# Transposes of q, k and x moved from TensorE to DMA, in a sliding-window attention followed by an MLP

## Chip, cores, metric

One core of one Trainium2 chip. All kernels of one comparison ran on the same chip beside the kernel before; the experiments used two chips, with medians of the kernel before of 362.0 to 362.5. SP below is SyncE, whose queue issues stores and DMA transposes; PSUM is where TensorE's products land; an eviction is ScalarE's copy of a finished PSUM bank to SBUF; the granted clock is TensorE's clock as a share of full speed.

## What is computed

```python
B, H, S, D = 8, 8, 576, 64
scores = q @ k.transpose(0, 1, 3, 2) / 8          # kept where 0 <= query - key < 64
attn   = softmax(scores) @ v
x      = attn.transpose(0, 2, 1, 3).reshape(4608, 512)
h      = x @ w_in                                  # 512 -> 2048
out    = (h - tanh(h)) @ w_out                     # 2048 -> 512
```

Inputs and output are float32; the kernel computes in bf16.

## The kernel before

The MLP runs in nine chunks of 512 tokens. A script counts half steps: an even one issues the four matmuls of `hp_mm` for one sixteenth of a chunk, an odd one the four of `yp_mm`, and attention work of later batches is put between them. A batch has 32 half steps. The parts that matter here:

```python
    def tr(g, which, bank, *engs):            # q or k of one pair of heads, on TensorE
        ...
        for e in range(E):
            nc.tensor.transpose(tp[:, e, :], src[:, e, :], ident[:P, :P])
        ...                                   # then copied from PSUM by ScalarE or VectorE
    def y_out(c, s):                          # one PSUM bank: the next yp_mm waits for this
        ysb = sm_pool.tile([128, d_model], F32, tag="ysb", name="ysb")
        nc.scalar.activation(ysb, ps[:, yp_bank(c, s), :], ACT.Copy)
        ...
    for g in range(3 * NP, B * NP):           # pairs of heads from the fourth batch on
        b, pr = divmod(g, NP)
        a = 8 * g - 48
        at(a - 7, cast, g, "q")
        at(a - 5, cast, g, "k")
        at(a, tr, g, "q", 3, nc.scalar, nc.vector)
        at(a + 2, tr, g, "k", 3, nc.scalar)
        for i in range(3):
            at(a + 5 + 2 * i, scores, g, i, 4)
        ...
        if pr % 2 == 1:
            at(a + 20, x_tr, b, pr // 2, 0, 4, 3)
            at(a + 22, x_tr, b, pr // 2, 4, NJ, 3)
        if pr == 0:
            at(32 * b - 78, load_v_all, b)    # GpSimd's software queue, casts f32 to bf16
            at(32 * b - 64, load_all, b, "q")
            at(32 * b - 63, load_all, b, "k")
    ...
        if h % 2 == 0:                        # order inside a half step
            if sy % 4 == 0 and 0 < n - LAG <= 16 * NC:
                y_out(*divmod((n - LAG) // 4 - 1, 4))
            if 0 <= c < NC:
                hidden = hp_mm(c, m)
        elif 0 <= cy < NC:
            yp_mm(cy, sy)
        for fn in items.get(h, []):
            fn[0](*fn[1:])
```

The softmax here doesn't subtract the row's maximum and nothing guards it: scores larger than these inputs give would overflow.

## Time and profile before

| | before |
|---|---|
| median, later runs of the same comparison included | 361.9 us |
| TensorE busy | 326.2 us of 362.1 |
| hardware-issued DMA | 17.69 MB |
| software-issued DMA (loads with a cast) | 17.90 MB |

The prediction shows the lines that tell what bounds it.

And one line in order of time, the eviction of y that precedes the q transposes at 151.46 us which the prediction shows:

```profile
151.19 0.59 ACT L283 ACTIVATE ysb<-ps 128x512 f32<-128x512 f32 x1
```

It ends at 151.78; the MLP matmuls that write the same PSUM bank start at 151.83.

### The profile page before, as it was taken

The page shows a single profiled execution, that of the slowest core. Times are in us where ns is not written, and L with a number is a line of the kernel's source. Part 1 is how long each engine was busy: PE and PEld are TensorE (multiplying, and loading weights), DVE is VectorE, ACT ScalarE, POOL GpSimd, SP SyncE. Part 2 cuts the span into 40 slices and gives each one's busy share as a digit, 9 for nine tenths or more (in the row PEclk, how much of TensorE's full clock was granted, in tenths as well). Part 3 has the DMA queues.
Part 4 walks back from the last instruction along what each step waited for, and adds up shares of the span by engine and source line. Part 5 has one row for each costly group of instructions (what it writes and reads, how often), then busy time and mean ns, then how long its engine had stood idle before and what let it go on. Part 6 is the DMA issues. An engine that isn't in the chain of part 4 may idle for free.

```text
span 362.1 us, 6043 instructions
## 1 busy us (share of the span) xinstructions
PE 326.2 (90%) x2329; PEld 189.5 (52%) x2329; DVE 214.7 (59%) x352; ACT 192.8 (53%) x355; POOL 103.6 (29%) x136
## 2 busy tenths in 40 slices
PE   0538667889999999999999999999999999999995
PEld 0438345655555555555555555555555544444442
DVE  3418657775676776767677767677676633443300
ACT  2536364876656656565656555655564444443421
POOL 7809522806319309312830272110000000000000
PEclk9999998999999999999999999999999999999999
DMA  8899992377876567655935592250000010010012
GB/s 158 128 218 200 216 222 54 54 137 114 202 155 92 97 163 123 129 99 121 139 84 108 128 129 74 58 127 31 30 32 29 31 58 29 31 57 29 31 67 78
DMA packets 31948, 36.76 MB, mean 102 GB/s; under 512 B 3472, under 2 KB 25872, under 8 KB 31536
## 3 DMA queue, kind: packets, MB, share of 16 engines
q0 software_dynamic: 20384, 17.90, 32.7%
q1 hardware_dynamic: 10904, 17.69, 17.0%
q10 hardware_dynamic: 632, 0.79, 0.7%
q8 instruction: 18, 0.29, 0.4%
q14 instruction: 10, 0.08, 0.1%
HBM read 36.70 MB, written 9.44 MB: 127 GB/s over the span
## 4 chain that ended last, share of the span: by engine, by line
PE 73%; DMA 15%; issue 5%; POOL 3%; ACT 2%; DVE 2%; SPq 0%; POOLq 0%; ACTq 0%; DVEq 0%
PE ps L278 32%; PE ps L259 29%; DMA vw<-vb 7%; DMA kall<-in_k_dram 4%; PE ps L224 4%; PE ps L197 3%; PE ps L210 3%; DMA vall<-in_v_dram 2%; PE ps L241 2%; DMA vw<-vw 1%; POOL kb L81 1%; POOL vb L81 1%; DVE qt L81 1%; ACT th L262 1%; POOL qb L81 0%
## 5 line engine op out<-in xcount | busy, mean ns | idle before, releaser
L259 PE MATMUL ps<-xT,wi 128*128 128x512 bf16 x576 | 148.2, 381 | 1.0 <-DVE gT L268 0.9
L278 PE MATMUL ps<-w_out_sb,gT 128*128 128x512 bf16 x576 | 145.2, 379 | 0.2 <-ACT ysb L283 0.2
L268 DVE TENSOR_TENSOR gT<-ps,th 128x512 bf16<-128x512 f32 x144 | 98.9, 690 | 74.2 <-ACT th L262 73.0
L262 ACT ACTIVATE th<-ps 128x512 f32<-128x512 f32 x144 | 86.0, 598 | 85.4 <-PE ps L259 84.1
L259 PEld LDWEIGHTS <-wi 128*128 128x128 bf16 x576 | 61.3, 114 | 47.0 <-issue 2.7
L278 PEld LDWEIGHTS <-gT 128*128 128x128 bf16 x576 | 53.6, 98 | 51.3 <-issue 0.5
L214 ACT ACTIVATE pt<-ps 128x384 bf16<-128x384 f32 x96 | 46.9, 491 | 48.5 <-PE ps L210 37.7
L81 POOL COPY vb<-vall 72x1024 bf16<-72x1024 bf16 x28 | 29.4, 1060 | 71.3 <-DMA vw<-vb 53.9
L235 DVE TENSOR_TENSOR xs<-ps,rc 64x576 bf16<-64x576 f32 x64 | 48.3, 755 | 1.5
L210 PE MATMUL ps<-qt,kt 128*128 128x128 bf16 x288 | 37.3, 230 | 5.6 <-ACT pt L214 3.1
L224 PE MATMUL ps<-vw,pt 128*128 128x130 bf16 x288 | 30.6, 229 | 8.5 <-DVE vw L133 7.1
L224 PEld LDWEIGHTS <-pt 128*128 128x128 bf16 x288 | 22.7, 102 | 22.5 <-issue 7.6
L81 POOL COPY qb<-qall 96x768 bf16<-96x768 bf16 x27 | 22.9, 848 | 36.2 <-PE ps L197 22.9
L81 DVE COPY qt<-ps 64x576 bf16<-64x576 bf16 x33 | 25.0, 757 | 12.9 <-ACT qt L79 8.3
L81 POOL COPY kb<-kall 96x768 bf16<-96x768 bf16 x28 | 23.6, 847 | 28.9 <-DMA kall<-in_k_dram 11.1
L210 PEld LDWEIGHTS <-kt 128*128 128x128 bf16 x288 | 25.0, 104 | 10.8 <-ACT kt L79 2.4
L283 ACT ACTIVATE ysb<-ps 128x512 f32<-128x512 f32 x36 | 21.4, 594 | 15.1 <-PE ps L278 15.1
L81 DVE COPY xT<-ps 128x512 bf16<-128x512 bf16 (+4 forms) x35 | 12.1, 368 | 16.8 <-PE ps L241 16.8
L197 PE MATMUL ps<-ident,qb 96*128 96x96 bf16 x192 | 14.4, 215 | 7.9 <-DVE qb L81 7.7
L79 ACT ACTIVATE qt<-ps 64x576 bf16<-64x576 bf16 x31 | 19.7, 635 | 3.5 <-PE ps L197 1.9
L79 ACT ACTIVATE kt<-ps 128x576 bf16<-128x576 bf16 x30 | 19.4, 645 | 2.6 <-PE ps L197 1.5
L197 PE MATMUL ps<-ident,kb 96*128 96x96 bf16 x192 | 14.4, 214 | 5.7 <-ACT kb L79 4.6
(47 smaller groups left out, 148.0 us busy)
## 6 DMA issues: line engine op xcount, KB each, us to landing
out_dram<-ysb SPq DMA_DIRECT2D x36, 256.0 KB
vw<-vb SPq DMA_DIRECT2D x67, 65.0 KB
vall<-in_v_dram POOLq DMA_DIRECT2D x7, 576.0 KB, 9.2
kall<-in_k_dram POOLq DMA_DIRECT2D x7, 576.0 KB, 10.2
qall<-in_q_dram POOLq DMA_DIRECT2D x7, 576.0 KB, 6.3
vw<-vw SPq DMA_DIRECT2D x6, 520.0 KB
w_out_sb<-in_moe_w_out_dram POOLq DMA_DIRECT2D x4, 512.0 KB, 13.3
wi<-in_moe_w_in_dram POOLq DMA_DIRECT2D x2, 512.0 KB, 14.0
```

The costliest lines, as they stand in the source:

```text
L79: nc.scalar.activation(o, i, ACT.Copy)
L81: eng.tensor_copy(o, i)
L197: nc.tensor.transpose(tp[:, e, :], src[:, e, :], ident[:P, :P])
L210: nc.tensor.matmul(sp[:, i, :], kT[g % NR][:, 64 * j:64 * j + 128], qT[g % NR][:, :, 64 * j:64 * j + 64], start=True, stop=g >= 2 * NP)
L214: nc.scalar.activation(PT[g % NPT][:, 3 * grp:3 * grp + 3, :], sp, ACT.Exp, scale=scale)
L224: nc.tensor.matmul(ps[:, 5 + grp, 130 * i:130 * i + 130], PT[g % NPT][:, j, :], vw[b % 2][:, j, 2 * pr:2 * pr + 2, :], start=True, stop=True)
L235: nc.vector.tensor_tensor(xo[r, :, :, pr, :], ov[r, :, :, h, 0:D], rc[r].to_broadcast([64, 3, 3, 64]), ALU.mult)
L259: nc.tensor.matmul(hp, w_in_tile(ki, m), chunk_tile(c)[:, ki, :], start=(ki == 0), stop=(ki == 3))
L262: nc.scalar.activation(th, hp, ACT.Tanh)
L268: nc.vector.tensor_tensor(gT[c][:, m, :], hp, th, ALU.subtract)
L278: nc.tensor.matmul(yp, gT[c][:, m, s * 128:(s + 1) * 128], w_out_sb[:, m, :], start=(m == 0), stop=(m == M - 1))
L283: nc.scalar.activation(ysb, ps[:, yp_bank(c, s), :], ACT.Copy)
```

## The change

TensorE bounds the middle, so its transposes are given to DMA: two pairs of heads are cast into one tile, written to DRAM scratch, and read back transposed; x is transposed from SBUF to SBUF. k is used as it lands; q is copied on VectorE into the block form with zeros. So that the data are early enough, q and k are loaded ten half steps earlier, and the attention work of the later batches starts two half steps earlier. The script of the first three batches is reordered.

```diff
+    def cast2(g, n):
+        i = g % 2
+        if i == 0:
+            two[n] = two_pool.tile([P, E, 2, 2, D], BF16, tag=n, name=n + "b2")
+        nc.gpsimd.tensor_copy(two[n][:, :, i].rearrange("p e h d -> p h e d"), ...)
+    def bounce(n):
+        t = dram.tile([S, 256], BF16, tag=n, name=n + "d")
+        nc.sync.dma_start(out=t.rearrange("(p e) c -> p (e c)", e=E), in_=...)
+    def tr2(g, n):
+        o = qT2[g // 2 % 2] if n == "q" else kT2[g // 2 % 2][:, :, 64:]
+        nc.sync.dma_start(out=o, in_=two.pop(n), transpose=True)
+    def x_dma(b): ...                  # the same from xs into the chunk's tile
+    def blocks(g):
+        for h in range(2):
+            r = slice(64 * h, 64 * h + 64)
+            nc.vector.tensor_copy(qT[g % NR][r, h], qT2[g // 2 % 2][r, g % 2])
...
-        a = 8 * g - 48
-        at(a, tr, g, "q", 3, nc.scalar, nc.vector)
-        at(a + 2, tr, g, "k", 3, nc.scalar)
+        a = 8 * g - 50
+        if pr % 2 == 0:
+            for i, n in enumerate("qk"):
+                at(a - 15 + 2 * i, cast2, g, n)
+                at(a - 14 + 2 * i, cast2, g + 1, n)
+                at(a - 12 + 2 * i, bounce, n)
+                at(a - 7 + 2 * i, tr2, g, n)
+        at(a + 2, blocks, g)
...
+        if pr == NP - 1:
+            at(a + 18, x_dma, b)
...
-            at(32 * b - 64, load_all, b, "q")
-            at(32 * b - 63, load_all, b, "k")
+            at(32 * b - 74, load_all, b, "q")
+            at(32 * b - 73, load_all, b, "k")
```

Cut: the reordered script, the constants of the new tiles, the new layout of the chunk's tile.

## The prediction

> **What bounds the kernel now.** I first read the head of the page for the busy shares, then the busy times in five stretches, and last the order of the TensorE's work in time.
>
> ```profile
> span 362.1 us, 6043 instructions
> PE 326.2 (90%) x2329; PEld 189.5 (52%) x2329; DVE 214.7 (59%) x352; ACT 192.8 (53%) x355; POOL 103.6 (29%) x136
> ...
> PE 73%; DMA 15%; issue 5%; POOL 3%; ACT 2%; DVE 2%; SPq 0%; POOLq 0%; ACTq 0%; DVEq 0%
> ```
>
> TensorE is busy for 90% of the span, and the chain that ended last runs through it for 73%. An average hides stages, so I asked for stretches of 35.10 us from 110 us on:
>
> ```profile
> core 0: us, PE busy (x) PEld busy (x) DVE busy (x) ACT busy (x) POOL busy (x), PEclk, DMA share, GB/s
> 110.00:145.10 35.10, 35.10 (x267) 20.61 (x266) 24.66 (x41) 21.63 (x42) 18.99 (x23) 1.00 0.68 124
> 145.10:180.20 35.10, 35.10 (x267) 20.63 (x266) 25.07 (x42) 21.15 (x41) 13.29 (x16) 1.00 0.64 120
> 180.20:215.30 35.10, 35.10 (x269) 20.57 (x266) 25.00 (x42) 21.15 (x41) 12.22 (x15) 1.00 0.58 110
> ```
>
> The first figure after the stretch is its length, the next TensorE's busy time: it never rests. VectorE is busy for 71%, ScalarE for 60%, the DMA engines for about two thirds. The same 267 to 269 matmuls recur, so one batch takes 35.1 us. A busy TensorE could still be one whose modelled ends overlap a wait, so I checked the starts:
>
> ```profile
> 151.46 0.42 PE L197 MATMUL ps<-ident,qb 96*128 96x96 bf16 x6
> 151.83 1.02 PE L278 MATMUL ps<-w_out_sb,gT 128*128 128x512 bf16 x4
> 152.69 0.33 PE L210 MATMUL ps<-qt,kt 128*128 128x128 bf16 x3
> 152.85 1.03 PE L259 MATMUL ps<-xT,wi 128*128 128x512 bf16 x4
> 153.72 0.42 PE L197 MATMUL ps<-ident,kb 96*128 96x96 bf16 x6
> 153.97 1.03 PE L278 MATMUL ps<-w_out_sb,gT 128*128 128x512 bf16 x4
> ...
> 166.53 0.44 PE L241 MATMUL ps<-ident,xs 128*128 128x128 bf16 x5
> 166.81 0.33 PE L224 MATMUL ps<-vw,pt 128*128 128x130 bf16 x3
> ```
>
> The columns are start, duration, engine, line. From start to start, four 512-column matmuls take 0.86 us, three score matmuls 0.165, six q transposes 0.37, six k transposes 0.25, five x transposes 0.28 (56 ns each). A batch then needs 128 x 0.2155 = 27.6 us of the MLP, 4 pairs of heads x 18 x 0.055 = 4.0 of scores and products with v, 4 x 0.62 = 2.5 of q and k transposes, 18 x 0.056 = 1.0 of x transposes: 35.1 us, just the measured period. The middle of the kernel is bounded by what TensorE has to issue, and by nothing else. The first 110 us are not: TensorE stands idle for some 32 us there, waiting for loads, casts and the copies of v.
>
> **What the Trainium skill says.** "VectorE: DVE Perf Modes", section "The three transpose paths", gives a 128x128 bf16 transpose as 390 ns on TensorE and 1309 ns by the DMA crossbar. The trace has a mean of 219 ns for an x transpose and 56 ns from one to the next, so a latency isn't what one costs in a stream; nothing before shows the DMA form. "DMA: Bandwidth & Descriptors", section "Latency and other measured facts", gives DMA transposes 261 GB/s with a non-contiguous middle dimension and some 350 to 400 when contiguous. No run shows that yet. The same page, section "Two DMAs through the same engine are not ordered", makes the issuing engine wait for the first DMA's completion before it issues one that reads its data: here the write to scratch and the transpose that reads it are two full latencies in series, and the SP queue, in which both stand, waits between them. Section "Issuing engines are not separate DMA queues" says that all queues share 16 DMA engines. The page of the kernel before agrees insofar as its loads slow down together: q lands in 6.3 us, k, issued next, in 10.2.
>
> **The change part by part.** Units of the script are half steps, 32 to a batch: 35.1/32 = 1.10 us each before.
>
> Removed from TensorE, for five batches: 20 pairs of q and k transposes x 0.62 = 12.4 us, and 90 x transposes x 0.056 = 5.0 us; in all 17.4 us. All of it lies in the stage where TensorE never rests, so all is on the path. The order of instructions confirms the counts: q and k transposes fall from 192 to 72 each, x transposes from 144 to 54, and nothing is added to TensorE. The first MLP matmul now reads its tokens as eight pieces of 64 columns. I give that no cost: score matmuls already read q in two pieces of 64 and start 55 ns apart, like the x transposes with a contiguous 128.
>
> VectorE loses 20 q copies of 0.76 us and some 8 us of x copies, and gains 40 block copies of 64x576 bf16 within SBUF. A cast-free copy of 96x768 took 0.35 us there, so one should take 0.27 us: 11 us added, 23 removed. ScalarE loses 20 x (0.64 + 0.64) = 26 us. Neither bounds this stage; GpSimd keeps the same number of casts.
>
> Added to DMA per batch: four writes of 576x256 bf16 (295 KB), four transposes of as much, and 590 KB of x, hence 2.95 MB. At 261 GB/s a q or k transpose needs an estimated 1.1 us (that page), x 2.3 us, and a fixed latency besides.
>
> Do they come in time? For a pair the script casts at -15, writes from -12, transposes q at -7 and wants it at +2, nine half steps later; k has ten. With a batch of 31.6 us a half step is 0.99 us, so nine are 9 us; two casts of 0.83 us, a write and a transpose of perhaps 3 us each need some 8 of the 17 us from the first cast to the use. GpSimd already waited up to 6.6 us for a q load; even that fits. x is tighter: its transpose is issued at 32b-8 behind a q transpose, and the chunk that reads it begins at 32b, some 8 us later. Its first part covers 5, 4, 3, 2 and 1 windows of 64 KB for batches 3 to 7: 328 KB at worst. I expect 3 us for the q transpose ahead of it and 3 to 4 for itself, so it just makes it, with a loss of a few us over the five batches where it doesn't: 3 us in expectation.
>
> The script of the first 110 us is reordered too, with the same work in it. It may give or take 4 us; without a reason for a sign I take 0.5 us of gain. Loads of batches 3 and later start ten half steps earlier, more load on busy DMA engines in the part that waits for DMA.
>
> Sum: 362.0 - 17.4 + 3 - 0.5 = 347 us.
>
> **Rivals.** (1) The DMA engines become the bound. From the queue table, hardware-issued DMA moved 17.69 MB in 17.0% of the span, 61.5 us of all 16 engines, so 288 GB/s. The added 2.95 MB are at that rate 10.2 us per batch on top of a DMA share of about 0.6 x 35.1 = 21 us: 31 us in a batch of 31.6. For it speaks this sum; against it, that the share reached 1.24 with 222 GB/s in the first 50 us, so 1.0 is no wall, and that loads are far ahead. If transposes ran at half that rate, TensorE would wait several us a batch and the gain would shrink to nothing: 352 to 365 us. Were each 128x128 block to cost its 1309 ns in series, a batch would need 54 x 1.309 = 71 us and the kernel would be far slower; I hold that for a latency and give it 3%.
>
> (2) A wait for x takes the place of the transposes removed, once a batch, at the first MLP matmul of a chunk. Three us late in each of five batches is 15 us back: 360 us. For it: 8 us of lead, the SP queue in which output stores and a q transpose stand ahead; against it: the first part shrinks from batch to batch.
>
> (3) Head-of-line blocking on SP: the shift of v waits for nine copies, an output waits for its eviction, and both hold up the transposes behind them. The slack of some 8 us per pair speaks against more than single waits: 349 to 352.
>
> (4) All is hidden and the start gets better as well: 341 to 344.
>
> **Range and chances.** The plain case (all hidden, or late by 5 us at most in sum) gives 342 to 350 and I hold it at 62%; a part of the gain returned, 350 to 358, at 20%; most of it or more returned, at 18%. The bounds of 2% are 354.8 and 369.2 us. Range 341 to 360; faster 0.74, same 0.17, slower 0.09.
>
> **What would show it.** Right: TensorE still 100% busy in the middle at about 31.6 us a batch; its matmul count lower by 330; MLP matmuls still 0.86 us per four; no wait at the score matmuls on the q copies or on DMA into k, no wait over 1 us at the first MLP matmul of a chunk on DMA into x; DMA share of about 0.9 in that stage. Wrong: idle of TensorE in front of scores or of a chunk's first MLP matmul with a DMA as releaser (rivals 1 to 3; all late means 1, only x means 2), MLP matmuls further apart than 216 ns (the pieces of 64 cost something), or a first 110 us that is longer by more than 4 us.

## More of the kernel before

The metric is the device time of one execution in microseconds; a median is over all four runs of a kernel, and three medians (said there) include one slow run.

The page's 40 slices (TensorE's busy tenths, then the mean busy share of the 16 DMA engines) and its DMA queues (packets, MB, share of the span):

```profile
PE   0538667889999999999999999999999999999995
DMA  8899992377876567655935592250000010010012
...
q0 software_dynamic: 20384, 17.90, 32.7%
q1 hardware_dynamic: 10904, 17.69, 17.0%
```

TensorE reads 9 from the tenth slice on; DMA has peaks at the loads and gaps between them.

## The result

380.8 us (379.4 to 382.3, four runs) against 361.9: 1.052 times the time, 95% interval 1.048 to 1.057. Slower; 347 was predicted, 341 to 360 the range. Ratios here are the mean of one kernel's fast runs over the mean of the other's of the same rounds, so not quite the ratio of the medians.

The changed kernel's page, with the lines that answer to those of before:

```profile
span 379.9 us, 5318 instructions
PE 317.7 (84%) x1968; PEld 175.3 (46%) x1999; DVE 205.7 (54%) x344; ACT 171.7 (45%) x316; POOL 104.2 (27%) x138
PE   1546879869838995889697979899999999999995
DMA  8999994976994698879979697966830131001012
...
q1 hardware_dynamic: 48520, 32.30, 35.8%
q0 software_dynamic: 20432, 17.97, 32.1%
...
PE 52%; DMA 30%; ACT 6%; POOL 4%; issue 4%; DVE 2%; SPq 1%; POOLq 0%; ACTq 0%; DVEq 0%
```

TensorE did lose work (330 weight loads fewer, as predicted; the count of matmuls falls by 31 more, which are records of MLP matmuls missing from the trace; 8.5 us less busy), but the span grew: its row has gaps in the middle, where before all slices read 9. DMA is now busy nearly everywhere up to the 29th slice. Its hardware queues moved 14.6 MB more, and their share of the span rose from 17.0% of 362.1 to 35.8% of 379.9, by 74.4 us of all 16 engines: 196 GB/s, not the 288 that the prediction took.

Where the time went is best read from the progress of the MLP. This table is worked out from the traces: the start of ScalarE's tanh of a half step, in us, for the kernel before, the changed one, and some of the experiments below. Kernels that are still the same up to half step 40 differ there by up to 2 us (80.57 in the changed one, 82.68 in no_v), so smaller differences before half step 64 mean nothing.

| half step | before | changed | new script alone | changed, no loads | spread | k alone by DMA |
|---|---|---|---|---|---|---|
| 40 | 86.60 | 80.57 | 80.96 | 81.57 | 82.27 | 82.12 |
| 64 | 116.55 | 122.56 | 111.18 | 114.81 | 117.22 | 113.82 |
| 160 | 222.00 | 243.02 | 216.62 | 214.14 | 225.62 | 216.35 |
| 208 | 274.75 | 293.28 | 269.37 | 263.84 | 275.92 | 267.55 |
| 286 | 343.63 | 361.50 | 338.26 | 332.05 | 344.14 | 336.43 |

The changed kernel is 6 us ahead at half step 40, 6 us behind at 64, 21 at 160, and gains 3 back from there, when the loads are over. Its waits of TensorE for DMA (the waits view: in total, times, longest, in us):

```profile
PE ps L252 <- DMA kt<-kd: 11.4, 5, 3.9
PE ps L274 <- DMA vw<-vw: 8.2, 2, 5.0
PE ps L307 <- DMA xT<-xs: 4.9, 3, 2.3
```

L252 are the scores, L274 the products with v, L307 the first half of the MLP. One of the five waits for k, in order of time:

```profile
125.88 1.54 SPq L231 DMA_TRANSPOSE qt<-qd  x1
129.00 0.83 POOL L122 DMA_DIRECT2D vall<-in_v_dram  x1
129.82 0.77 POOL L103 DMA_DIRECT2D qall<-in_q_dram  x1
130.58 0.84 POOL L103 DMA_DIRECT2D kall<-in_k_dram  x1
131.38 5.56 SPq L231 DMA_TRANSPOSE kt<-kd  x1
146.09 0.50 PE L252 MATMUL ps<-qt,kt 128*128 128x128 bf16 x3 [3.95 <-DMA kt<-kd]
```

The q transpose at 125.88 has its last packet at 128.62, 2.7 us after its issue (packet times are from the trace). Then GpSimd, whose next instructions these are and which here waits for nothing, issues the three loads of the next batch in one go, and the k transpose comes right behind them: its issue alone takes 5.56 us, its packets begin at 137.39 and end at 145.49, 14.1 us after the issue. Two more of the ten k transposes took 12.8 us, each beside loads; in all three SP issued k's transpose behind an output store, which in turn waits for an eviction, 4.6 to 7.5 us after q's. TensorE waits 3.95 us, and at the end of the wait its granted clock falls: 0.50 from 145.73 to 149.13 us, so the matmuls after the wait start slowly.

The transposes' packets have 256 bytes: 34,560 of them, 55.1 us of all engines by the sum of their times, 160 GB/s. The writes to scratch, 5.9 MB in packets of 3072 bytes, took 16.7 us, 353 GB/s.

One more reading, of the stretches without any late transpose. There eight half steps take 8.28 us (for example the tanh at half steps 176, 184, 192: 260.15, 268.43, 276.71). Before, 35.1 / 4 = 8.78. So the removed work is worth 0.49 us per pair of heads, 10 us in 20 pairs, and not the 17.4 of the prediction. The lines that tell why:

```profile
129.72 1.03 PE L307 MATMUL ps<-xT,wi 128*128 128x512 bf16 x4
129.91 0.49 ACT L254 ACTIVATE pt<-ps 128x384 bf16<-128x384 f32 x1 [0.43 <-PE ps L252]
130.30 0.59 ACT L332 ACTIVATE ysb<-ps 128x512 f32<-128x512 f32 x1
130.94 1.02 PE L327 MATMUL ps<-w_out_sb,gT 128*128 128x512 bf16 x4 [0.20 <-ACT ysb L332]
```

The four matmuls at 129.72 could be followed at 130.58, but the next four write the bank of y, which ScalarE is still emptying, because an exponential stands in front of it. They start at 130.94: 0.36 us are lost in every pair. Before, the six q transposes (0.25 us of issue, and 0.12 of waiting that the prediction took for issue) stood in just this gap.

### The profile page after: what moved, and what is told of

It is laid out like the page before. It is cut to its first block, busy times and chain, and to the rows that moved or that the text cites. A ratio compares the mean times of both kernels' runs of the same rounds, so it can differ in the third digit from the quotient of the medians.

```text
span 379.9 us, 5318 instructions
## 1 busy us (share of the span) xinstructions
PE 317.7 (84%) x1968; PEld 175.3 (46%) x1999; DVE 205.7 (54%) x344; ACT 171.7 (45%) x316; POOL 104.2 (27%) x138
## 3 DMA queue, kind: packets, MB, share of 16 engines
q1 hardware_dynamic: 48520, 32.30, 35.8%
## 4 chain that ended last, share of the span: by engine, by line
PE 52%; DMA 30%; ACT 6%; POOL 4%; issue 4%; DVE 2%; SPq 1%; POOLq 0%; ACTq 0%; DVEq 0%
PE ps L327 25%; PE ps L307 21%; DMA kt<-kd 14%; DMA vw<-vb 10%; DMA vw<-vw 4%; PE ps L274 3%; ACT ysb L332 2%; PE ps L252 2%; DMA xT<-xs 2%; POOL vb L86 2%; DMA vall<-in_v_dram 1%; ACT th L311 1%; DVE gT L317 1%; ACT pt L264 1%; SPq L238 1%
## 5 line engine op out<-in xcount | busy, mean ns | idle before, releaser
L307 PE MATMUL ps<-xT,wi 128*128 128x512 bf16 x576 | 152.4, 389 | 6.1 <-DMA xT<-xs 4.9
L327 PE MATMUL ps<-w_out_sb,gT 128*128 128x512 bf16 x545 | 141.7, 383 | 5.4 <-ACT ysb L332 3.3
L327 PEld LDWEIGHTS <-gT 128*128 128x128 bf16 x576 | 56.2, 99 | 69.0 <-issue 11.6
L307 PEld LDWEIGHTS <-wi 128*128 128x128 bf16 x576 | 61.8, 115 | 54.3 <-issue 6.3
L274 PE MATMUL ps<-vw,pt 128*128 128x130 bf16 x288 | 31.4, 232 | 15.9 <-DMA vw<-vw 8.2
L274 PEld LDWEIGHTS <-pt 128*128 128x128 bf16 x288 | 23.2, 103 | 32.6 <-DMA vw<-vw 8.7
L252 PE MATMUL ps<-qt,kt 128*128 128x128 bf16 x180 | 20.4, 224 | 11.4 <-DMA kt<-kd 11.4
L220 POOL COPY qb<-qall 96x768 bf16<-96x768 bf16 x20 | 15.9, 824 | 38.2 <-DMA qd<-qb 36.5
L252 PEld LDWEIGHTS <-kt 128*128 128x128 bf16 x180 | 13.7, 100 | 17.4 <-DMA kt<-kd 12.2
L268 DVE TENSOR_TENSOR pt<-pt,ps 128x1152 bf16<-128x1152 bf16 x24 | 17.9, 744 | 1.2 <-ACT pt L264 1.2
L246 DVE COPY qt<-qt 64x576 bf16<-64x576 bf16 x40 | 17.9, 447 | 0.3
L220 POOL COPY kb<-kall 96x768 bf16<-96x768 bf16 x20 | 15.9, 824 | 2.7 <-DMA kall<-in_k_dram 2.7
L281 DVE RECIPROCAL rc<-ps 128x9 f32<-128x9 f32 x32 | 6.8, 213 | 12.6 <-PE ps L274 12.6
```

The costliest lines, as they stand in the source:

```text
L220: nc.gpsimd.tensor_copy(two[n][:, :, i].rearrange("p e h d -> p h e d"), stage.pop((g, n)).rearrange("p h (e d) -> p h e d", d=D))
L252: nc.tensor.matmul(sp[:, w, :], kT2[g // 2 % 2][:, g % 2, 64 * j:64 * j + 128], qT[g % NR][:, :, 64 * j:64 * j + 64], start=True, stop=True)
L274: nc.tensor.matmul(ps[:, 5 + grp, 130 * i:130 * i + 130], PT[g % NPT][:, j, :], vw[b % 2][:, j, 2 * pr:2 * pr + 2, :], start=True, stop=True)
L307: nc.tensor.matmul(hp, w_in_tile(ki, m), chunk_tile(c)[:, :, ki % 2, 64 * (ki // 2):64 * (ki // 2) + 64], start=(ki == 0), stop=(ki == 3))
L327: nc.tensor.matmul(yp, gT[c][:, m, s * 128:(s + 1) * 128], w_out_sb[:, m, :], start=(m == 0), stop=(m == M - 1))
```

## The experiments

Theory 1: the DMA transposes come late because they share the DMA engines with the loads. Theory 2: they are slow by themselves or in their queue. And apart from both: the q transposes were free.

**no_loads.** Its output is wrong, which doesn't matter for the time.

```diff
     def load_all(b, n):
-        t = all_pool.tile(...); nc.gpsimd.dma_start(out=t, in_=...)
+        if b <= 3:
+            t = all_pool.tile(...); nc.gpsimd.dma_start(out=t, in_=...); kept[n] = t
+        t = kept[n]                    # v alike
```

> Wrong result on purpose: the changed kernel, but from the fifth batch on q, k and v are not loaded; the fourth batch's are used again. Theory 1 (the transposes come late because they share the DMA engines with the three software-queue loads, which were moved in front of them): the waits for DMA into k and xT in the middle vanish, a transpose takes 2 to 3 us from issue to its last packet, eight half steps take 8.3 us throughout, and the time falls by some 22 us of waits in the middle, to 352 to 359 us. Theory 2 (the transposes, or their issue on the SP queue, are slow by themselves): within 3 us of the changed kernel, 378 to 382.

354.6 us, ratio 0.976 (0.967 to 0.985), all as Theory 1 had it. The stretch from 120 to 250 us of the kernel before, of the changed one and of this run (length, TensorE's busy time, ..., granted clock, DMA share, GB/s):

```profile
120.00:250.00 130.00, 130.00 (x983) 76.18 (x982) 92.33 (x153) 78.41 (x148) 43.96 (x52) 1.00 0.54 108
```

```profile
120.00:250.00 130.00, 110.67 (x646) 58.35 (x658) 78.47 (x132) 56.19 (x107) 41.26 (x50) 0.96 0.88 170
```

```profile
120.00:250.00 130.00, 126.01 (x767) 67.86 (x780) 89.27 (x160) 66.91 (x126) 32.56 (x38) 1.00 0.67 154
```

TensorE idles 19 us of 130 in the changed kernel, 4 in this one, which are the gaps at the bank of y. The waits are most of what loads cost: from half step 64 to the end the changed kernel loses 21.7 us on this run, and its waits for k and x sum to 16.2. The granted clock was 0.50 in three stretches of 3.4 us at the ends of such waits (from 145.73, 162.80 and 227.65 us), and 1.00 here throughout; by estimate that is another 5 us. The k transpose that took 14 us is issued here at 123.64, and its packets end at 126.83:

```profile
123.64 1.31 SPq L239 DMA_TRANSPOSE kt<-kd  x1
```

Theory 2 falls: the same transposes in the same queue are quick without the loads. From half step 64 to the end this run gains 9.8 us on the kernel before, just the 10 us worked out above. GpSimd also does less here, but in the middle it was never what TensorE waited for.

**plan_only.** The changed file with the loop of the kernel before for the later batches.

> The new script of the first part, with q, k and x of all batches transposed on TensorE and loads where they were before. Theory 1: the new script itself gains the 6 us that the changed kernel is ahead by at half step 40, and the loss from half step 40 to 64 comes from the earlier loads and the first DMA transposes: about 356 us. Rival: the new script causes the loss up to half step 64 (6 us behind there): about 368 us.

358.2 us, ratio 0.986 (0.978 to 0.994). The table's column stays 5.4 us ahead from half step 56 to the end: the new script is a gain, and what the changed kernel loses between 40 and 64 is not due to it.

**qk_only** and **x_only.** One of the two transfers alone.

```diff
 qk_only, in the changed kernel:            x_only, in the changed kernel:
-        if pr == NP - 1:                   -        cast2, bounce, tr2, blocks, scores2
-            at(a + 18, x_dma, b)           +        at(a - 7, cast, g, "q"); at(a - 5, cast, g, "k")
+        if pr % 2 == 1:                    +        at(a, tr, g, "q", 3, nc.scalar, nc.vector)
+            at(a + 20, x_tr, ...)          +        at(a + 2, tr, g, "k", 3, nc.scalar)
+            at(a + 22, x_tr, ...)          +        loads of q, k at 32 * b - 64, - 63
```

> q and k by DMA as in the changed kernel, x by TensorE again. Theory 1: the k waits stay, the x waits (5 us) go and 5 us of x transposes come back: 377 to 383. Rival (the x transposes in the same queue hold up the k transposes and are the cause): 358 to 366.

381.4 us, ratio 1.051 (1.041 to 1.061): the path of q and k, with its earlier loads, is enough for the whole loss.

> x by DMA as in the changed kernel, q and k by TensorE with their loads two half steps before their old place, the new script. Theory 1: the 5 us of x transposes are saved on top of the script's gain, less a wait of 0 to 1 us per batch for x: 351 to 356. Rival (x waits take the place of the transposes whatever the q, k path): 358 to 364.

360.4 us, ratio 0.992 (0.985 to 1.000), in the rival's range, a miss of 4 us. (Its loads stand at their old place, not two half steps earlier as the expectation says; the rest of the loop is two earlier.) The rival's reason is not borne out, though: TensorE's matmuls wait for x only 2.1 us in all. The run loses 3.6 us between half steps 40 and 64, where plan_only loses none. The attention work of the later batches begins two half steps earlier than in plan_only, which was a second difference; that this is the cause was not tested. From 64 to the end it gains 2.4 us, half of the 5 that x transposes take.

**before_no_q** and **before_no_k.** Their outputs are wrong, which doesn't matter for the times. The check of results does not notice q or k of another batch (q and k are normal draws times 0.1, so the scores are about 0.01 and the softmax is nearly even). "Correct" therefore says little of the paths of q and k.

```diff
 before_no_q                                        before_no_k
-        at(a - 7, cast, g, "q")                    -        at(a - 5, cast, g, "k")
-        at(a, tr, g, "q", 3, nc.scalar, nc.vector) -        at(a + 2, tr, g, "k", 3, nc.scalar)
```

> Wrong result on purpose: the kernel before, without the casts, transposes and copies of q from the fourth batch on. My prediction counted 0.37 us for each of these 20 groups of six transposes. If it had been right, the time falls by 7.4 us, to 354.5. If they only fill a wait for the eviction of y that is there anyway, the time falls by less than 1.5 us, 360.5 to 362.

361.7 us, ratio 0.999 (0.996 to 1.003). From half step 64 to the end its progress stays 2.5 us ahead of the kernel before, to 0.02 us: 120 transposes, their casts and their copies taken away, and nothing gained. The wait is now open:

```profile
157.24 0.59 ACT L283 ACTIVATE ysb<-ps 128x512 f32<-128x512 f32 x1
157.89 1.02 PE L278 MATMUL ps<-w_out_sb,gT 128*128 128x512 bf16 x4 [0.20 <-ACT ysb L283]
```

> Wrong result on purpose: the same for k. These 20 groups have no such wait behind them: the time falls by 20 times 0.25 = 5 us, to 356 to 358 us, under either theory.

357.9 us, ratio 0.990 (0.984 to 0.996); from half step 64 to the end 4.6 us are gained, against 5.0 worked out. So of a pair's 0.62 us only k's 0.25 were a cost.

**gated** and **gated_y.** The loads held back to the times between transposes.

```diff
+    def gate(h):
+        c, m = divmod(h // 2 - 1, M)
+        nc.gpsimd.tensor_copy(scr, gT[c][0:1, m, 0:1])     # one element
-            at(32 * b - 78, load_v_all, b); at(32 * b - 74, load_all, b, "q"); at(32 * b - 73, load_all, b, "k")
+            h_v, h_qk = (18 if b == 3 else 32 * b - 86), 32 * b - 70
+            at(h_v, gate, h_v);   at(h_v, load_v_all, b)
+            at(h_qk, gate, h_qk); at(h_qk, load_all, b, "q"); at(h_qk, load_all, b, "k")
```

gated_y also has `scores2` at `a + (5, 7, 10)[i]`.

> The changed kernel, correct, with the loads of q, k and v held back by a one-element copy on GpSimd that waits for the MLP: v ten half steps into a batch's period, q and k twenty-six, that is, between the transposes and not beside them. Theory 1 (contention with the loads): the k waits go and the time falls to 351 to 358 us, as without the loads. Rival (the DMA engines are simply full, whatever the order): 368 us or more.

385.0 us, ratio 1.064 (1.059 to 1.069): my remedy failed, in the rival's range. The waits for k are gone, as planned, but in their place:

```profile
PE ps L312 <- DMA xT<-xs: 22.4, 4, 7.7
```

The bursts now fall on q and x. The q transpose meant for half step 87 was issued at 147.51 us, near half step 90, behind the writes to scratch and the shift of v, and just after the loads at 146.02 and 146.79; the x transposes, 151.05 and 155.98, stood behind it.

> As the run before, and the last third of the scores one half step later, so that no exponential stands on ScalarE in front of the eviction of y. Theory: eight half steps take 7.9 us in place of 8.28, 20 times 0.37 = 7 us less than the run before: 344 to 351. Rival (the 0.37 us belong to something else): within 2 us of it.

389.9 us (one of four runs slow), ratio 1.072 (1.065 to 1.080); neither expectation was met. Locally the edit does what it should: from half step 144 to 152 it takes 7.91 us where gated takes 8.29. A TensorE that is ahead only waits longer.

**k_dma**, **kx_dma**, **k_dma_y.** A smaller dose: q back on TensorE, where it was free.

```diff
         at(a - 7, cast, g, "q")
-        at(a - 5, cast, g, "k")
         at(a, tr, g, "q", 3, nc.scalar, nc.vector)
-        at(a + 2, tr, g, "k", 3, nc.scalar)
+        if pr % 2 == 0:
+            at(a - 15, cast2, g, "k"); at(a - 14, cast2, g + 1, "k")
+            at(a - 12, bounce, "k");   at(a - 7, tr2, g, "k")
-            at(32 * b - 63, load_all, b, "k")
+            at(32 * b - 73, load_all, b, "k")      # q stays at - 64; a = 8 * g - 48
```

kx_dma also has x_dma at `a + 16`; k_dma_y has `scores2` at `a + (5, 8, 9)[i]`.

> Correct. The new script, and from the fourth batch on only k goes by DMA; q, whose transposes were free, and x stay on TensorE. The k load stays ten half steps early, q's goes back. DMA work per batch, from the packets' times of the changed kernel: about 20 us of loads, v copies and outputs, 1.7 of writes and 3.7 of transposes, 25 in a period of 34. Theory 1 (what hurt was too much DMA work at once, not the DMA transpose as such): 358.2 of the script alone less 20 times 0.25 us, 350 to 356. Rival (any transpose by DMA in this queue is late): 360 or more.

355.5 us, ratio 0.979 (0.974 to 0.984): 2.7 us below the script alone in the median, but that ran on the other chip, and the intervals of the two ratios overlap. From half step 64 on 4.5 us are gained on the kernel before, all of k's share, and TensorE is full again:

```profile
120.00:250.00 130.00, 129.20 (x913) 74.88 (x926) 95.53 (x160) 72.42 (x137) 41.34 (x49) 1.00 0.73 141
```

> Correct. As the run before, and x by DMA too: another 3.7 us of DMA transposes per batch, 29 in a period of 33. If that still fits: 5 us less than the run before, 346 to 352. If not, TensorE waits for x and it is no better than the run before.

367.7 us, ratio 1.016 (1.010 to 1.021). The added x transposes put the DMA share at 0.87, and TensorE waits:

```profile
PE ps L301 <- DMA xT<-xs: 10.9, 3, 6.3
```

So a DMA transpose is no loss as such; the second dose is. The success of k_dma itself is not the dose alone, though: its q load stands apart again (v and k issued at 122.85 and 123.67 us, q at 140.73), so its burst is smaller too.

> Correct. Only k by DMA, and the second third of the scores one half step later, so that y is evicted at once. There the q transposes still fill most of that gap; 0.12 us per pair of heads are left: 2 to 3 us less than the 355.5 of the run with k alone, 352 to 354. Rival: no gain.

354.2 us, ratio 0.979 (0.975 to 0.983): 1.2 us less in the median than k_dma, about half of what was expected, and the two ratios' intervals overlap, so a gain of the edit is not shown. It is the lowest median of a kernel that computes everything.

**no_loads_y** and **no_v.** Wrong results: no_loads with the scores edit of gated_y, and the changed kernel without the loads of v alone.

> Wrong result on purpose: the changed kernel without loads from the fifth batch on, and the last third of the scores one half step later, so that no exponential stands in front of the eviction of y. Held-back loads had shown 7.91 us per eight half steps locally with this edit, but given back in waits. Without loads it should stay: 20 times 0.37 us less than the 354.6 without the edit, 345 to 349. Rival: 353 or more.

351.5 us (one of four runs slow), ratio 0.967 (0.959 to 0.974). Between the two outcomes: from half step 64 to the end it gains 15.3 us on the kernel before, 5.5 more than no_loads, so the wait for y is real; the total loses some of it in the first 64 half steps.

> Wrong result on purpose: the changed kernel without the loads of v alone from the fifth batch on, 5 of the 13 us of DMA time that the three loads take. If the waits come from the amount of DMA work in front of the transposes, they shrink by 40% or more: 362 to 371 us. If they come from the start of any load beside a transpose, 376 or more.

364.7 us, ratio 1.005 (0.999 to 1.010). 5 of 13 us of load time per batch removed, and some 16 of the 26 us of loss against no_loads vanish: the waits follow the amount of load work in front of the transposes.

**spread** and **spread_y.** The same bytes, in pieces.

```diff
-                at(32 * b - 78, load_v_all, b); ...
+                for n, leads in dict(v=(88, 85, 80, 75), q=(83, 78, 67, 62), k=(73, 70, 59, 57)).items():
+                    for i, lead in enumerate(leads):        # fifth batch on; each behind a gate
+                        at(32 * b - lead, piece, 32 * b - lead, b, n, i)
```

> Correct. The changed kernel, with the loads of each batch from the fifth on in twelve pieces of one pair of heads, about 2.6 half steps apart, each held back by a one-element copy. The same bytes, but at most about 1 us of load in front of a transpose. If the burst is the cause: the middle runs at 8.3 us per eight half steps, 352 to 360 us. If it is the amount of DMA work per batch (about 34 us at the packets' times in a period of 33): 368 or more.

367.0 us, ratio 1.015 (1.010 to 1.020), correct. Neither number was met, and it lies near the second: breaking the burst gives 14 us back of the 26 that no_loads gives. The DMA share is 0.99, which does not prove the engines full (it is 1.30 from 140 to 146 us of the changed kernel). The waits for k are gone but not those for x:

```profile
120.00:250.00 130.00, 118.83 (x720) 63.66 (x734) 84.79 (x146) 61.87 (x116) 67.39 (x118) 0.99 0.99 188
```

```profile
PE ps L316 <- DMA xT<-xs: 7.2, 3, 3.1
```

> Correct. As spread, with the last third of the scores one half step later. If spread is free of waits: 4 to 7 us less than it. If DMA work is the bound: no gain, within 3 us of it.

364.0 us (one of four runs slow), ratio 1.003 (0.996 to 1.009), 3 us less than spread, on the border of the two expectations: no better than the kernel before.

## Why the prediction was wrong

**What bounds the kernel.** Right for the kernel before, as far as it went: before_no_k and k_dma show that k's transposes removed from TensorE in the middle are time removed. It knew that a busy TensorE can hide a wait under a modelled end, and looked at the starts, but took every distance between them for issue. The 0.37 us of six q transposes against 0.25 of six k transposes stood in the quoted lines, and the difference was a wait.

**Removed from TensorE: 17.4 us.** This term failed. 10 us is what it is worth (no_loads: 9.8). The k transposes cost what was worked out (4.6 of 5.0 us); the q transposes cost nothing (before_no_q), since they stood in the shadow of the eviction of y. That is 7.4 us of gain that never was.

**Do they come in time?** This is the step that failed with the larger size. "A write and a transpose of perhaps 3 us each" holds for an undisturbed transpose (2.7 us). Beside the loads k's took 12.8 to 14.1 in three of ten cases, and ten half steps weren't enough. "That loads are far ahead", which I held against rival 1, was the cause: GpSimd runs ahead of the script and issues v, q and k of the next batch in 2.4 us, in front of a k transpose. The change itself, by moving q and k ten half steps up, put all three together; before, v's loads stood alone (153.23 us and 187.95, for example). No run left both loads at their old place with q and k by DMA, so what this move cost by itself is not shown.

**Rival 1** named the right resource, and its loss was still sized too small (352 to 365 us). Its sum used 288 GB/s of the hardware queues before; the added transfers ran at 196. At that rate 2.95 MB are 15 us a batch and not 10.2, so the sum would have been 36 us in a batch of 31.6 (an estimate). Spread, with the same bytes in pieces, gives 14 of the 26 us back, and no_v, with less of them, 16: how the loads stand counts, and how much they are, and the runs don't part the two further. Rival 2, the wait for x, is real (4.9 us) and small in the changed kernel; it becomes the main wait as soon as k is cured. Rival 3 is seen in part: TensorE waited twice for the shift of v itself, 8.2 us in all, in the stage from half step 40 to 64.

**MLP reading in eight pieces:** no cost, as predicted; four matmuls stay 0.86 us apart. **Block copies:** 0.45 us in the mean, not 0.27; off the path.

**The first 110 us.** The new script gained 5.4 us, not 0.5, and the new path lost 12 us between half steps 40 and 64. no_loads loses only 3 there, so the larger part is again the loads of the fifth batch; the rest, with one wait of 2.8 us for the shift of v, was not taken apart by a run of its own; x_only, which shares with it the start two half steps earlier, loses 3.6 there.

Open: whether some order of the same transfers would beat k_dma_y. Two orders were tried and neither did; none put k's transposes ahead of the output store that stands in front of them on SP.

## What to carry to other kernels

An operation on the busiest engine may stand in front of a wait that is there anyway; look at what ended just before its successor could start (here an eviction on another engine) before counting its removal as gain. When a second user is put on the DMA engines, ask which transfers will stand in front of it at the moment of issue; here an engine with nothing to wait for sent its prefetches at the worst moment. A part of such a change can be worth keeping: k alone by DMA gained what k cost, and the rest gave it back.

## What the Trainium skill lacked or had wrong

- "DMA: Bandwidth & Descriptors", section "Latency and other measured facts": 261 GB/s, or 350 to 400, for DMA transposes. Here a transpose of 295 KB with no load beside it had its packets within 1.1 to 1.9 us (155 to 259 GB/s), one beside loads needed 8.1 us (36 GB/s), and over the whole kernel the packets' times give 160 GB/s.
- "Advanced Engine Details and Errata", section "X-Bar Transpose (TRN2)", has transposes as fast as regular DMAs. Here: 160 GB/s in packets of 256 bytes, against 353 GB/s for the writes to scratch in packets of 3072.
- "DMA: Bandwidth & Descriptors", section "Issuing engines are not separate DMA queues", calls the issue usually small relative to the DMA. Here the SP queue was held 1.3 us by an undisturbed transpose of 1.5 us of packets, and 5.56 us behind loads.
- "VectorE: DVE Perf Modes", section "The three transpose paths", gives 1309 ns for a 128x128 block by DMA. A block's share of an undisturbed transpose of 576x256 (4.5 times 2 blocks) was 2.7 / 9 = 0.30 us, issue included.
- No page that I read says that TensorE work may be free because it fills the wait for a PSUM bank's eviction: 120 transposes removed, 0.0 us gained in the middle.
